# Top-k attention and ELU feed-forward: the products with the values placed behind the first feed-forward share of a step, and one subtraction for both rows

## The chip, the core and the metric

The kernel runs on one core of a Trainium2 chip. The core has five engines with queues of their own: TensorE (PE in the profile, PEld for its weight loads), VectorE (DVE), ScalarE (ACT), GpSimd (POOL) and SyncE (SP), which here only starts DMAs. The metric is the device time of one execution in microseconds (us). The engines work through their queues in the order in which the program was written, and wait for one another by semaphores.

## The reference

Inputs are `q`, `k`, `v` of shape (8, 8, 576, 64) (batches, heads, rows, head size), `w_in` (512, 2048) and `w_out` (2048, 512). Cut to what matters:

```
scores = q @ k.T / sqrt(64)                      # per batch and head, 576 x 576
kth    = 32nd largest of each row
scores = where(scores >= kth, scores, -1e9)
scores = scores - max(scores, -1)
attn   = exp(scores); attn /= sum(attn, -1) + 1e-9
x      = (attn @ v), heads side by side          # 4608 x 512
h      = x @ w_in
g      = where(h > 0, h, exp(min(h, 0)) - 1)     # ELU
out    = g @ w_out                               # 4608 x 512
```

## The kernel before, in words

**Steps.** A *tile* is 128 query rows of a batch (five per batch; the fifth, the remainder, holds the 64 last rows and takes two head pairs at once). A *step* is one tile with two heads, `i` = 0 and 1 (a remainder step packs four heads' 64 rows into the same shape); there are 144. The tile `sc` holds the scores of a step as 128 x 2 x 576. The main loop runs over `n` and works on four steps at once: it makes the scores of step `n + 2` (`scores`, products L329 into PSUM `scps`, ACT's copies L337), selects the threshold of step `n` on DVE (`select`), masks step `n - 1` (`mask`) and normalises it at the end (`normalise`), and turns step `n - 2` (`turn`).

**Select** finds the 32 largest of each row: four times MAX8 (L349, L363) with three MATCH_REPLACE8 between (L356). `u.first` (tile `m1`) keeps the first eight, `u.last` (tile `m4`) the last eight, so that `u.last[:, i, 7]` is the 32nd largest and `u.first[:, i, 0]` the largest. It is a generator with four passes; `next(passes)` emits one.

**Mask** works on one head `i`: POOL forms `gap`, the threshold less the largest score (L384, one column), ACT applies a very steep Prelu around the threshold (L385) and then Exp with `gap` as bias and the row's sum as by-product (L386). In the first steps (`early`, up to step 8) ACT forms `gap` itself (L382). Four-column tile `den` holds the two sums and the two gaps.

**Normalise** is POOL alone: L396 to L401 make the reciprocals on 128 x 2, L403 multiplies the two rows of 576.

**Turn** transposes the nine 128-column chunks of `sc` on PE (L422, five in `eps` and `scps`, then four in `eps`), and ACT copies them to `et` (L423, three copies). When the last tile of a group (one or two tiles of one head pair) is turned, the group goes onto `closing`, and the next step calls **attend**: ten products with the values (L448, PSUM `avps`; twenty for the remainder), each a 128 x 64 weight, and ACT's copy to `xT` (L475, in `finish`). When a block of one to three tiles is complete, its feed-forward pieces join the list `ffn`.

**Feed-forward pieces.** A block has 16 hidden pieces and four projection pieces per tile. A hidden piece is four products (L523, PSUM `hps`, two buffers); where a PSUM bank is full ACT takes Relu of both signs (L533, L536), and for every pair of pieces Exp (L538) and, later on, a Copy with bias -1 (L542); POOL adds the halves (L493; in the first steps and for the last block DVE does, L495), the *gate*, some shares later. A projection piece is four products (L551, PSUM `ops`); after the fourth piece ACT copies the result (L560) and SP writes it out (L563). In the profile each of these products shows as two records, so that a piece is "x8", the values of a group "x20" or "x40" and the scores of a step "x8" or "x16".

**Feed.** `feed(n, 0.25)` is called four times a step. It closes gates that are old enough and emits as many pieces as a plan of shares allows, made before the loop from estimated costs. The order of instructions on each engine is just the order of these calls, since the kernel schedules by hand. Buffers: five `sc`, two `et`, four of each small tile; `avps` and `eps` share two PSUM buffers, and the last chunk of the first transposes lies in the bank of the second head's scores.

The start of a step reads (L686 to L693):

```python
        if ahead and n > 1:
            scores(ahead)
        while closing:
            attend(closing.pop(0))
        next(passes)
        feed(n, 0.25)
        if prev:
            mask(prev, 0, n <= tight)
```

Of the kernel before, what the change touches and what calls it, by code (L numbers as in the profile page):

```python
# [9 lines left out]
ALU = mybir.AluOpType  # L10
FP32 = mybir.dt.float32
# [69 lines left out]
def kernel(  # L81
# [9 lines left out]
    nc = tc.nc  # L91
    P = nc.NUM_PARTITIONS
# [18 lines left out]
    def pool(name, bufs, **kw):  # L111
        return ctx.enter_context(tc.tile_pool(name=name, bufs=bufs, **kw))
# [6 lines left out]
    small = pool("small", 4)  # L119
# [8 lines left out]
    early = raws.enter_context(tc.tile_pool(name="early", bufs=1))  # L128
# [73 lines left out]
    def settle():  # L202

        if decode or late or blocks[0].left or any(x[3] == 0 for x in ffn):
            return
        raws.close()
        late["f"] = ctx.enter_context(tc.tile_pool(name="f", bufs=2))
        late["g"] = ctx.enter_context(tc.tile_pool(name="g", bufs=2))
        late["x"] = ctx.enter_context(tc.tile_pool(name="xt", bufs=2))
        late["in"] = ctx.enter_context(tc.tile_pool(name="in", bufs=2))  # L210
# [100 lines left out]
    def turn_qk(whole=False):  # L311
        while turning:
            if next(turning[0], turning) is turning:
                turning.pop(0)
            elif not whole:
                return
# [3 lines left out]
    def scores(u):  # L320

        u.sc = scpool.tile([P, 2, S], FP32, tag="sc", name="sc")
        q0 = (QUERIES if u.t.b == 0 else S) + u.t.qt * P
        for half in range(2):
            for h, i, rows in u.heads:
                kq = kqT[u.t.b, h // 2]
                part = slice(i * D, (i + 1) * D)
                k0 = (KEYS if i == 0 and u.t.b == 0 else 0) + half * HS
                nc.tensor.matmul(  # L329
                    wide[i][rows, half, 0:HS],  # L330
                    kq[part, q0 : q0 + u.t.ql],
                    kq[part, k0 : k0 + HS],
                    start=True,
                    stop=True,
                )
        for i in range(2):
            nc.scalar.activation(  # L337
                u.sc[:, i, :].rearrange("p (a s) -> p a s", a=2),
                wide[i][:, :, 0:HS], AF.Copy, scale=scale,
            )  # L340

    def select(u, more=False):

        u.first = small.tile([P, 2, 8], FP32, tag="m1", name="m1")
        u.last = small.tile([P, 2, 8], FP32, tag="m4", name="m4")
        cur = [u.sc[:, i, :] for i in range(2)]
        found = [u.first[:, i, :] for i in range(2)]
        for i in range(2):
            nc.vector.max(found[i], cur[i])  # L349
        if more:  # L350
            hook()
        yield
        wk = [wkpool.tile([P, S], FP32, tag=f"wk{i}", name="wk")[:] for i in range(2)]
        for r in range(TOP_K // 8 - 1):
            for i in range(2):
                nc.vector.match_replace(wk[i], found[i], cur[i], TAKEN)  # L356
            cur = wk
            for i in range(2):
                if r < TOP_K // 8 - 2:
                    found[i] = small.tile([P, 8], FP32, tag=f"m{i}", name="m")[:]  # L360
                else:
                    found[i] = u.last[:, i, :]
                nc.vector.max(found[i], cur[i])  # L363
            hook()
            yield

    def mask(u, i, early=False):

        if u.masked:
            return
        if i == 0:
            u.den = small.tile([P, 4], FP32, tag="den", name="den")
        u.masked = i == 1
        sc, low, top = u.sc[:, i, :], u.last[:, i, 7:8], u.first[:, i, 0:1]
        gap = u.den[:, 2 + i : 3 + i]  # L380
        if early:
            nc.scalar.activation(gap, top, AF.Prelu, scale=-1.0, bias=low, alpha=1.0)  # L382
        else:
            nc.gpsimd.tensor_tensor(gap, low, top, ALU.subtract)  # L384
        nc.scalar.activation(sc, sc, AF.Prelu, scale=-1.0, bias=low, alpha=1.0 / STEEP)  # L385
        nc.scalar.activation(  # L386
            sc, sc, AF.Exp, scale=-STEEP, bias=gap, accum_out=u.den[:, i : i + 1]
        )
# [43 lines left out]
    def attend(g):  # L432
        t = g.tiles[0]
        ps = ps_t.tile([P, JP], FP32, tag="t", name="avps")
        n = P if t.rem else sum(x.ql for x in g.tiles)
        for k in range(2 if t.rem else 1):
            hp = 2 * g.hp + k if t.rem else g.hp
            vt = vT[t.b, hp]
            for c in range(J + 1):
                for i in range(2):  # L440
                    chunk = J if c == J else i * (J + 1) + c
                    w = g.et[:, chunk, :, :].rearrange("p a q -> p (a q)")
                    cols = slice(0, n)
                    if t.rem:
                        c0 = R * (k if i == 0 else 1 - k)
                        w = w[:, c0 : c0 + R]
                        cols = slice(k * R, (k + 1) * R)
                    nc.tensor.matmul(  # L448
                        ps[i * D : (i + 1) * D, cols],
                        vt[:, 2 * J + i if c == J else i * J + c, :],  # L450
                        w,
                        start=(c == 0),
                        stop=(c == J),
                    )
        if t.rem:
            finish(t.block, 2, slice(2 * g.hp, 2 * g.hp + 2), t.cols,
                   ps[:, 0:n].rearrange("p (a q) -> p a q", a=2))
            return
        c0 = 0
        tiles = list(g.tiles)  # L460
        while tiles:
            blk, lo, parts = tiles[0].block, tiles[0].cols.start, 0
            while tiles and tiles[0].block is blk:
                parts += 1
                hi = tiles.pop(0).cols.stop
            finish(blk, parts, g.hp, slice(lo, hi), ps[:, c0 : c0 + hi - lo])
            c0 += hi - lo
# [15 lines left out]
    def close_gates(keep=0, upto=None):  # L483

        while gates:
            put, group, dst, n, apart = gates[0]
            if put > place[0] - keep if upto is None else group > upto:
                return  # L490
            gates.pop(0)
            if apart:
                nc.gpsimd.tensor_tensor(dst, n, dst, ALU.add)  # L493
                continue
            nc.vector.scalar_tensor_tensor(  # L495
                out=dst, in0=n, scalar=-1.0, in1=dst, op0=ALU.add, op1=ALU.add
            )
# [81 lines left out]
    blocks, tight = [], 2 * NHP  # L579
    for b in range(B):  # L580
# [28 lines left out]
        for qts in order:  # L609
# [3 lines left out]
            for qt in qts:  # L613
                n = len(steps)
# [24 lines left out]
    def feed(n, share):  # L639

        place[0] += 1
        close_gates(2 if n > tight + 3 else 6)
        fed["at"] = max(fed["at"], n)
        ahead = [(w - fed["sum"]) / (x - fed["at"]) for x, w in due if x > fed["at"]]
        if ahead:
            fed["over"] += max(0.0, share * min(ahead))
        fed["at"] += share
        while ffn and decoded[0] >= ffn[0][1] and 0.5 * ffn[0][0] <= fed["over"]:
            cost, _, piece, _ = ffn.pop(0)
            fed["over"] -= cost  # L650
            fed["sum"] += cost
            piece()
            settle()
# [22 lines left out]
    def step(n):  # L676
        return steps[n] if 0 <= n < NS else None
# [3 lines left out]
    for n in range(NS + 3):  # L681
        for fn, args in todo.pop(n, []):
            fn(*args)
        ahead, cur, prev, done = step(n + 2), step(n), step(n - 1), step(n - 2)
        passes = select(cur, n < tight) if cur else iter(range(4))
        if ahead and n > 1:  # L686
            scores(ahead)
        while closing:
            attend(closing.pop(0))
        next(passes)  # L690
        feed(n, 0.25)
        if prev:
            mask(prev, 0, n <= tight)  # L693
        if n > 1:
            turn_qk()
        next(passes)
        feed(n, 0.25)
        if done:
            turn(done, main)
            turn(done, rest)  # L700
        if prev:
            mask(prev, 1, n <= tight)
        next(passes)
        feed(n, 0.25)
        if done:
            turn(done, other)
        next(passes)
        if prev:
            normalise(prev)
        feed(n, 0.25)  # L710
        turn_qk(True)
        if n < 2:
            scores(ahead)
# [36 lines left out]
```

## Time and profile before

| what | us |
|---|---|
| median of 3 runs | 1633.88 (1632.33 to 1633.99) |
| the profiled execution, its own time | 1633.17 |
| span of that execution's instructions | 1631.4 |
| PE busy | 1569.5 (96%) |
| DVE busy | 1454.4 (89%) |
| ACT busy | 1174.6 (72%) |
| POOL busy | 711.6 (44%) |

The span runs from the first to the last instruction; the execution's own time has 1.8 us more around it. "Busy" of PE is modelled: products are pipelined, and one that stands in the pipeline and waits can count as busy. A line `PE avps L448 <- ACT et L423: 19.7, 26, 2.4` of the waits means that PE sat idle for 19.7 us in total, 26 times, 2.4 us at most, before a product into `avps` of line 448, until ACT's write of `et` at line 423. In a timeline line the first number is the start and the second the length of a run of like instructions; idle time before it stands in brackets. The granted clock of TensorE is 1.00 in nearly all of the span after the first 125 us.

### The profile page before, as it was taken

What the parts mean: (1) busy time and instruction counts of PE and PEld (TensorE: products, weight loads), DVE (VectorE), ACT (ScalarE), POOL (GpSimd) and SP (SyncE); (2) the same over time, 40 slices, a digit from 0 to 9 for tenths busy, and PEclk for the clock granted to TensorE, in tenths of its full rate; (3) what the DMA queues carried; (4) which work ended last, traced back from release to release, by engine and by line L of the source; (5) the groups of instructions that cost most, each with busy time, mean ns of one, the idle gap of its engine ahead of it and who ended that gap; (6) DMA issues with size and microseconds to landing.
All of it is one profiled execution on the core that took longest, in us unless ns stands there. A gap on an engine that the chain in (4) does not pass through costs nothing.

```text
span 1631.4 us, 25301 instructions
## 1 busy us (share of the span) xinstructions
PE 1569.5 (96%) x8276; PEld 1004.7 (62%) x8276; DVE 1454.4 (89%) x2980; ACT 1174.6 (72%) x2369; POOL 711.6 (44%) x1535
## 2 busy tenths in 40 slices
PE   4789999999999999999999999999999999999999
PEld 2477666766665757555566666655557575755564
DVE  7899999999999999999999699999999599998000
ACT  6987777877776868778577786868668695958521
POOL 4983345444443444444344443535435353534300
PEclk9779999999999999999999999999999999999999
DMA  8521310012100310022000200012100201000000
GB/s 243 187 79 36 65 37 1 7 22 45 43 1 19 54 37 7 7 40 46 23 8 15 55 21 25 1 28 45 36 14 1 43 1 36 1 13 1 7 14 13
DMA packets 188035, 56.17 MB, mean 34 GB/s; under 512 B 178176, under 2 KB 179200, under 8 KB 187904
## 3 DMA queue, kind: packets, MB, share of 16 engines
q1 hardware_dynamic: 186704, 54.26, 14.1%
q8 instruction: 66, 1.08, 0.3%
q14 instruction: 65, 0.53, 0.1%
q10 hardware_dynamic: 1200, 0.30, 0.1%
HBM read 45.09 MB, written 9.44 MB: 33 GB/s over the span
## 4 chain that ended last, share of the span: by engine, by line
PE 74%; ACT 14%; DVE 5%; POOL 3%; issue 1%; SPq 1%; DMA 1%; ACTq 0%; DVEq 0%; POOLq 0%
PE ops L551 29%; PE hps L523 22%; PE avps L448 10%; PE scps L329 7%; PE eps L422 5%; ACT sc L386 3%; DVE wk L356 2%; ACT sc L385 2%; ACT et L423 2%; DVE m L363 2%; ACT n L542 1%; ACT n L533 1%; ACT n L538 1%; ACT gT L536 1%; POOL sc L403 1%
## 5 line engine op out<-in xcount | busy, mean ns | idle before, releaser
L363 DVE MAX8 m<-wk 128x8 f32<-128x576 f32 x864 | 611.2, 751 | 0.3 <-POOL den L384 0.3
L523 PE MATMUL hps<-xT,w_in 128*128 128x256 f32 (+2 forms) x2432 | 542.9, 373 | 0.0
L551 PE MATMUL ops<-w_out,gT 128*128 128x512 f32 x1152 | 522.5, 598 | 0.0
L523 PEld LDWEIGHTS hps<-xT,w_in 128*128 128x128 f32 x2432 | 404.9, 192 | 97.4 <-issue 25.4
L356 DVE MATCH_REPLACE8 wk<-m,wk 128x576 f32<-128x576 f32 x576 | 424.5, 747 | 0.0
L551 PEld LDWEIGHTS ops<-w_out,gT 128*128 128x128 f32 x1152 | 208.6, 190 | 231.7 <-issue 230.6
L396 POOL TENSOR_SCALAR dene<-den 128x2 f32<-128x2 f32 x144 | 32.5, 225 | 693.1 <-ACT sc L386 692.5
L386 ACT ACTIVATE sc<-sc,den 128x576 f32<-128x576 f32 x288 | 223.4, 776 | 66.1 <-POOL den L384 44.4
L385 ACT ACTIVATE sc<-sc,m 128x576 f32<-128x576 f32 x288 | 225.0, 781 | 9.6 <-DVE m L363 9.5
L337 ACT ACTIVATE sc<-scps 128x576 f32<-128x576 f32 x288 | 170.9, 646 | 77.8 <-PE scps L329 77.8
L448 PE MATMUL avps<-et,vT 128*64 128x256 f32 (+2 forms) x2080 | 205.6, 328 | 20.1 <-ACT et L423 19.7
L329 PE MATMUL scps<-kqT 64*128 64x288 f32 (+1 forms) x1280 | 199.9, 443 | 25.1 <-ACT kqT L305 12.6
L349 DVE MAX8 m<-sc 128x8 f32<-128x576 f32 x288 | 202.6, 747 | 20.6 <-ACT sc L337 20.6
L403 POOL TENSOR_SCALAR sc<-sc,rec 128x576 f32<-128x576 f32 x288 | 213.5, 751 | 14.9
L423 ACT COPY et<-eps 128x512 f32<-128x512 f32 x288 | 164.6, 571 | 66.2 <-PE eps L422 66.2
L356 DVE MATCH_REPLACE8 wk<-m,sc 128x576 f32<-128x576 f32 x288 | 212.2, 746 | 0.0
L448 PEld LDWEIGHTS avps<-et,vT 128*64 128x64 f32 x2080 | 128.0, 141 | 101.0 <-ACT et L423 34.2
L422 PEld LDWEIGHTS eps<-ident,sc 128*128 128x128 f32 x1152 | 143.4, 143 | 72.4 <-issue 53.9
L493 POOL TENSOR_TENSOR gT<-n,gT 128x512 f32<-128x512 f32 (+1 forms) x120 | 166.2, 1385 | 38.0 <-ACT n L542 38.0
L422 PE MATMUL eps<-ident,sc 128*128 128x128 f32 x1152 | 174.1, 277 | 0.1
L329 PEld LDWEIGHTS scps<-kqT 64*128 64x128 f32 (+1 forms) x1280 | 107.0, 182 | 102.5 <-issue 46.2
L533 ACT ACTIVATE n<-hps 128x512 f32<-128x512 f32 (+1 forms) x156 | 87.0, 558 | 58.0 <-PE hps L523 57.1
(45 smaller groups left out, 988.5 us busy)
## 6 DMA issues: line engine op xcount, KB each, us to landing
raw<-in_moe_w_in_dram SPq DMA_DIRECT2D x16, 512.0 KB, 4.9
vT<-in_v_dram SPq DMA_DIRECT2D x64, 128.0 KB, 2.4
raw<-in_moe_w_out_dram SPq DMA_DIRECT2D x16, 512.0 KB, 3.8
out_dram<-osb SPq DMA_DIRECT2D x32, 256.0 KB, 2.0
kin<-in_k_dram SPq DMA_DIRECT2D x112, 72.0 KB, 2.4
qin<-in_q_dram SPq DMA_DIRECT2D x112, 72.0 KB, 2.5
kin<-in_k_dram SPq DMA_DIRECT2D x8, 128.0 KB, 4.7
vT<-in_v_dram SPq DMA_DIRECT2D x64, 16.0 KB, 2.2
```

Source lines behind the costliest of these rows:

```text
L329: nc.tensor.matmul(wide[i][rows, half, 0:HS], kq[part, q0 : q0 + u.t.ql], kq[part, k0 : k0 + HS], start=True, stop=True,)
L349: nc.vector.max(found[i], cur[i])
L356: nc.vector.match_replace(wk[i], found[i], cur[i], TAKEN)
L363: nc.vector.max(found[i], cur[i])
L385: nc.scalar.activation(sc, sc, AF.Prelu, scale=-1.0, bias=low, alpha=1.0 / STEEP)
L386: nc.scalar.activation(sc, sc, AF.Exp, scale=-STEEP, bias=gap, accum_out=u.den[:, i : i + 1])
L403: nc.gpsimd.tensor_scalar(u.sc[:, i, :], u.sc[:, i, :], rec[:, i : i + 1], 1.0, ALU.mult, ALU.mult)
L422: nc.tensor.transpose(ps[:, c * P : (c + 1) * P], sc[:, c0 : c0 + P], ident[:])
L423: nc.scalar.copy(g.et[:, chunks, u.at, :], ps[:, 0 : n * P].rearrange("p (c q) -> p c q", c=n),)
L448: nc.tensor.matmul(ps[i * D : (i + 1) * D, cols], vt[:, 2 * J + i if c == J else i * J + c, :], w, start=(c == 0), stop=(c == J),)
L523: nc.tensor.matmul(blk.h[:, f % bank, :], w_in[:, i, f * P : (f + 1) * P], blk.xT[:, i, 0:n_tok], start=(i == 0), stop=(i == NC - 1),)
L551: nc.tensor.matmul(blk.o[:], blk.gT[f // NG][:, f % NG, s * P : (s + 1) * P], w_out[:, f, :], start=(f == 0), stop=(f == NF - 1),)
```

## The change

The call of `attend` moves from the place before the first pass and the first feed of a step to the place behind them. The subtraction that forms the gaps is taken out of `mask` for all steps that are not early and becomes one POOL operation on two columns, in a new function `spread`, called once a step ahead of the first pass. The tile `den` is then made in `spread`. Lines from 367 on move down by 7, those behind the mask's subtraction by 5, and those behind the moved call by 7 again; the prediction keeps to the numbers of the kernel before.

```diff
+    def spread(u):
+
+        u.den = small.tile([P, 4], FP32, tag="den", name="den")
+        nc.gpsimd.tensor_tensor(
+            u.den[:, 2:4], u.last[:, :, 7], u.first[:, :, 0], ALU.subtract
+        )
+
     def mask(u, i, early=False):
...
-        if i == 0:
+        if i == 0 and early:
             u.den = small.tile([P, 4], FP32, tag="den", name="den")
...
         if early:
             nc.scalar.activation(gap, top, AF.Prelu, scale=-1.0, bias=low, alpha=1.0)
-        else:
-            nc.gpsimd.tensor_tensor(gap, low, top, ALU.subtract)
...
         passes = select(cur, n < tight) if cur else iter(range(4))
         if ahead and n > 1:
             scores(ahead)
+        if prev and n > tight:
+            spread(prev)
+        next(passes)
+        feed(n, 0.25)
         while closing:
             attend(closing.pop(0))
-        next(passes)
-        feed(n, 0.25)
         if prev:
             mask(prev, 0, n <= tight)
```

## The prediction

> **What bounds the kernel now.** I read the page first: its busy shares and the chain that ended last.
>
> ```profile
> PE 1569.5 (96%) x8276; PEld 1004.7 (62%) x8276; DVE 1454.4 (89%) x2980; ACT 1174.6 (72%) x2369; POOL 711.6 (44%) x1535
> PE 74%; ACT 14%; DVE 5%; POOL 3%; issue 1%; SPq 1%; DMA 1%; ACTq 0%; DVEq 0%; POOLq 0%
> ```
>
> PE and DVE are both nearly full, so an average can't say which one sets the end. The windows by stage (PE, PEld, DVE, ACT, POOL busy) can:
>
> ```profile
> 125.00:437.00 312.00, 305.26 (x1988) 209.66 (x1987) 312.00 (x641) 232.81 (x473) 137.82 (x325) 1.00 0.17 32
> 437.00:600.00 163.00, 157.76 (x842) 101.91 (x842) 160.33 (x331) 123.33 (x249) 70.90 (x157) 0.99 0.12 24
> 900.00:1300.00 400.00, 398.69 (x2027) 246.47 (x2026) 366.94 (x755) 293.72 (x594) 171.61 (x390) 1.00 0.13 27
> ```
>
> Up to 437 us DVE has no idle time, and the first Prelu of a mask (L385) starts as soon as DVE has that step's threshold: DVE sets the pace there, and nothing saved on PE is worth anything. After 437 us L385 trails DVE's last MAX8 by 3 to 29 us (12.1 us at 1441), DVE idles, and PE sets the pace, in the order in which its instructions stand. So the sum is over PE's stops after 437 us. The list of waits names those that the change can touch (us in total, times, longest):
>
> ```profile
> ACT xT L475 <- PE avps L448: 51.9, 49, 2.7
> ACT sc L386 <- POOL den L384: 44.4, 49, 4.3
> DVE kqT L283 <- PE scps L329: 36.1, 3, 16.9
> PE avps L448 <- ACT et L423: 19.7, 26, 2.4
> ```
>
> The last one is on PE. This is its longest case in the timeline (start us, length):
>
> ```profile
> 450.80 0.89 PE L329 MATMUL scps<-kqT 64*128 64x288 f32 x4
> 451.61 0.65 PE L448 MATMUL avps<-et,vT 128*64 128x256 f32 x2
> 453.55 0.63 ACT L542 ACTIVATE n<-n 128x512 f32<-128x512 f32 x1
> 454.08 0.57 ACT L423 COPY et<-eps 128x512 f32<-128x512 f32 x1
> 454.70 1.55 PE L448 MATMUL avps<-et,vT 128*64 128x256 f32 x6 [2.44 <-ACT et L423]
> ```
>
> Two records of the values product start, then PE stands until ACT, late with feed-forward work, has copied the last transposes of the step before. The wait rows show only part of this, since a record that waits in the pipeline counts as busy. So I measured each values group from its first record to the next group: undisturbed it takes 2.31 us (1.31 with remainder tiles). What is above that, over the 60 groups from 431 us on, in order: 4.43, 0.93, 1.15, 0.98, 1.60, 0.53, 0.93, 0.45, 1.69, 0.39, then 0.44, 1.40, 0.39, 1.40 at 1100, 1121, 1146 and 1482 us, six of 0.53 to 0.57 (3.28 together), 0.14, 0.79 and 0.74 in the last three, and two of 0.08: 21.8 us.
>
> **The change, part by part.** *Values behind the first share.* In the changed program's order, 40 of the 60 groups get one piece of feed-forward products between scores and values that stood behind them before; of the last three, which follow no scores, two get a projection piece in front and one a second hidden piece. A piece lasts 1.73 us (hidden, two-slot block), 2.58 (three-slot) or 3.43 (projection). No product is added: the piece only runs while ACT finishes L423. Four stops have no piece in front after the change either and stay: 1.60, 0.53, 0.39 and 0.39, 2.9 us. Of the 4.43 only 1.83 to 1.93 is covered (two-slot piece), so 2.5 stays. All others are shorter than their cover. Gain: 21.8 - 2.9 - 2.5 = 16.4 us.
>
> What PE pays: the products use three array shapes, and each change of shape has a price.
>
> ```profile
> 1390.49 0.60 PE L422 MATMUL eps<-ident,sc 128*128 128x128 f32 x4
> ...
> 1391.04 1.89 PE L523 MATMUL hps<-xT,w_in 128*128 128x256 f32 x8
> 1392.76 0.60 PE L422 MATMUL eps<-ident,sc 128*128 128x128 f32 x4
> 1393.20 1.89 PE L523 MATMUL hps<-xT,w_in 128*128 128x256 f32 x8
> 1395.02 1.24 PE L329 MATMUL scps<-kqT 64*128 64x288 f32 x8
> 1396.19 2.38 PE L448 MATMUL avps<-et,vT 128*64 128x256 f32 x20
> ```
>
> The same piece takes 1.72 us from start to next start between transposes and 1.82 ahead of scores: 0.10 for leaving the full shape. Behind scores or values it also takes 0.10 more. Before, a step goes scores, values, full shape; after it goes scores, full, values, full: one visit more. Where full products follow the values (20 groups) that is 0.20 us, out and back in. Where transposes follow (20 groups) it is 0.15: 0.10, and 0.60 for 0.55 in the transposes. Sum: 20 x 0.20 + 20 x 0.15 = 7.0 us lost. No row shows a values group behind products without a stop; one (1512.9 us) takes 2.45, which may be a wait, so 0 to 0.14 more each, at most 5.6; I take 0, since 2.45 holds a copy that ended inside it.
>
> This is where the Trainium skill speaks against the change: TensorEngine Tiling (Array Packing), Key Properties, says that changing the tiling mode drains TensorE. The rows agree and give about 0.1 us. The page gives no length; with a free drain the sum would end at 1616.8 us, with the rows' price at 1623.8.
>
> *L475 behind the piece.* ACT's copy of the values now waits later, and L385, L386 and L423 are queued behind it; POOL's normalising waits for L386 and the transposes of the next step for POOL. Projection piece, worst: before, L475 at 1440.76, first mask done 1442.77, ACT idle 1.61 until L560 at 1444.38, second mask done 1447.26, POOL's L403 done 1450.78, next transposes at 1453.4: 2.6 us spare. A shift of 3.64 loses 1.61 in ACT's gap, 2.0 arrives, under 2.6. Hidden piece: the shift of 1.93 falls into ACT's wait for products before L533 (57.1 us over 48 times). Price 0; bound below in the rivals. The hidden products that moved ahead need their PSUM freed by L536, which ACT does before the L423 they now cover, so they don't stop in its place.
>
> *One subtraction for both rows.* 272 POOL operations of 189 ns become 136 on two columns; the nearest row is L399, 128x2, 196 ns: 51.4 us become 26.7 on an engine that is 44% busy. It also stands ahead of the gate additions (L493, 1.28 or 1.83 us) of its share, which now wait behind it for DVE; nobody is listed as waiting for L493. L386's 44.4 us are ACT idle, mostly not on the chain. After 437 us three chain pieces run L493, L384, L386 (471, 553, 736 us): at most 1.24 + 1.25 + 1.78 + 3 x 0.16 = 4.8 us, largely the same stops that I counted above. I take 0. A loss: one operation waits for the second row's MAX8 (0.66 us later) before the first row's Exp, while DVE leads; the first Prelu (0.78) hides it, and up to 437 us PE's order has room.
>
> *SP and the feed.* The pieces per step stay nearly the same; a block's pieces join one share later, output DMAs move by a share, neither on the chain.
>
> Sum against the profiled execution's own 1633.17 us (span 1631.4 and 1.8 around): 1633.17 - 16.4 + 7.0 = 1623.8. The median shown is 0.7 above that execution, which would make it 1624.5; I say 1624.0, between the two and nearer to the first.
>
> **Rivals.** *The crossings and small new waits eat it.* With 2.45 for each moved group it is 1623.8 + 5.6 = 1629.4, and with the stops moved to the next ACT copy instead of removed about 1633: no change. For: ACT is 72% busy and its queue decides the stops. Against: in 900 to 1300 us it is idle for 106 of 400.
>
> *DVE holds longer.* At 601 us L385 starts only 2.96 us behind DVE; PE's net gain by then is 5.0 - 1.5 = 3.5, DVE itself gains back up to 2.67 that it idles in L283. If that lead is used up, the 3.5 is lost: 1627.5. Against: 2.96 + 2.67 is more.
>
> *Slower: masks too late.* If ACT's gap doesn't absorb the shift, all 3.64 us arrives where 2.6 are spare, and the transposes wait 1.04 in each of the 20 groups that transposes follow: +20.8, less the net gain of 9.4: 1633.17 + 11.4 = 1644.6. It decides as soon as more than 2.6 us of the shift comes through; by the timeline 2.0 does.
>
> **Chances.** Forecast 0.70, DVE 0.08, eaten 0.12, late masks 0.10. A run can tell about 0.2% (3.3 us) from no change: faster 0.78, same 0.12, slower 0.10. Low end: no price for shapes, 1617. High end: 1629.4 from the 2.45 row, stretched to 1631 for part of the eaten case; late masks and the rest stay out.
>
> **What would show it.** Right: the wait of avps for L423 after 437 us falls from 7.6 us to under 3; hidden pieces of 1.93 between scores and values; L386's wait for POOL under 20 us; L396 idle unchanged; DVE's L283 wait smaller by about the gain. Wrong: transposes of eps or scps waiting for POOL's L403 by many us, ACT's L475 waits far above 52 us with PE stopping behind them, or values groups of 2.45 and more.

## The result, and the profile after

| kernel | median (range, executions), us | ratio to before, 95% interval |
|---|---|---|
| before | 1633.24 (1632.33 to 1633.99, 4) | |
| changed | 1616.49 (1616.20 to 1616.57, 4) | 0.9897 [0.988, 0.9915] |

The change gains 16.7 us by the medians, and 16.6 us by the two profiled executions (1633.17 and 1616.54, span 1614.3). The forecast was 9.4 us, and the time lies 0.5 us below the range: sign and mechanism were right, the size wasn't. In the kernel after, the lines named in the prediction stand lower: L384 is now L370 (`spread`), L385 and L386 are L390 and L391, L403 is L408, L422 and L423 are L427 and L428, L448 is L453, L475 is L480, L523 is L528, L551 is L556.

The page of the changed kernel, its busy shares and the chain that ended last:

```profile
PE 1563.4 (97%) x8276; PEld 993.3 (62%) x8276; DVE 1454.2 (90%) x2980; ACT 1175.2 (73%) x2369; POOL 695.1 (43%) x1399
PE 71%; DVE 20%; ACT 4%; issue 2%; POOL 1%; SPq 1%; DMA 1%; DVEq 0%; ACTq 0%; POOLq 0%
```

No engine works less but POOL (136 operations fewer) and PE, whose records hold fewer hidden waits. In the chain ACT went from 14% to 4% and DVE from 5% to 20%. The chain by stage shows where: between 330 and 437 us its largest lines were PE's before (L551 26.6%, L448 13.1%, L523 12.1%), and now they are DVE's (L356 38.1%, L363 29.5%, L349 11.0%).

The windows by stage (PE, PEld, DVE, ACT, POOL busy, granted clock):

```profile
125.00:437.00 312.00, 305.99 (x1968) 209.17 (x1968) 312.00 (x642) 233.15 (x475) 132.95 (x290) 0.99 0.17 32
437.00:600.00 163.00, 161.27 (x878) 103.14 (x876) 163.00 (x337) 125.74 (x253) 70.78 (x149) 1.00 0.14 27
900.00:1300.00 400.00, 400.00 (x2064) 248.16 (x2064) 380.75 (x782) 300.48 (x607) 168.03 (x354) 1.00 0.13 27
```

From 437 to 600 us DVE now has no idle time left (2.67 us before), and PE 1.73 us where it had 5.24; from 900 to 1300 us PE is never idle. The 0.99 in the first row is a half clock from 202.6 to 206.0 us, behind a stop of 1.94 us at the scores (L329 waits for ACT's L428) that the kernel before doesn't have there. The list of waits:

```profile
ACT xT L480 <- PE avps L453: 99.1, 63, 5.2
POOL den L370 <- DVE m L363: 72.2, 40, 4.1
ACT sc L391 <- POOL den L370: 37.5, 50, 4.4
DVE kqT L283 <- PE scps L329: 23.9, 2, 16.8
PE avps L453 <- ACT et L428: 5.7, 9, 1.0
```

The last line was 19.7 us. ACT now waits 99.1 us for the values products instead of 51.9, since its copy of them stands in front of its other work. From 428 us on PE has no listed wait for that copy. The longest stop of before, at 451 us, looks like this now (timeline):

```profile
449.31 1.99 PE L528 MATMUL hps<-xT,w_in 128*128 128x256 f32 x8
451.24 0.65 PE L453 MATMUL avps<-et,vT 128*64 128x256 f32 x2
451.73 0.57 ACT L428 COPY et<-eps 128x512 f32<-128x512 f32 x1
452.35 2.37 PE L453 MATMUL avps<-et,vT 128*64 128x256 f32 x18 [0.46 <-ACT et L428]
```

The hidden piece stands between scores and values, 1.93 us from its start to the values' start, and where 2.44 us of waiting were listed, 0.46 are left. The crossings between array shapes can be read in a stretch without stops:

```profile
1315.49 1.89 PE L528 MATMUL hps<-xT,w_in 128*128 128x256 f32 x8
1317.31 1.24 PE L329 MATMUL scps<-kqT 64*128 64x288 f32 x8
1318.48 1.99 PE L528 MATMUL hps<-xT,w_in 128*128 128x256 f32 x8
1320.41 2.38 PE L453 MATMUL avps<-et,vT 128*64 128x256 f32 x20
1322.72 1.99 PE L528 MATMUL hps<-xT,w_in 128*128 128x256 f32 x8
```

From start to start the piece takes 1.82 us ahead of the scores, 1.93 us behind them, and the values behind products take 2.31 us, not 2.45: the row of 2.45 us that stood as the rival's price was a wait. All 43 groups that now stand behind full products, but the one at 451 us, take their undisturbed length.

**The sum made again, from both traces.** I measured every PE group (scores, values, transposes) from 431 us (before) and 428.5 us (after) on, from its first record to the next group's, against its undisturbed length:

| us above the undisturbed length | before | after | gone |
|---|---|---|---|
| values | 21.8 | 4.0 | 17.8 |
| scores | 4.35 | 2.5 | 1.9 |
| transposes | 3.2 | 1.1 | 2.1 |
| all | 29.4 | 7.6 | 21.8 |

The visits changed as in the order: scores followed by full shape 45 to 85 times, full shape followed by values 3 to 43, scores followed by values 57 to 17. With the prices of the prediction that is 7.0 us, which leaves 14.8; and PE reaches the transposes of step 38 (at 437.6 us before) 1.9 us earlier. Together 16.7, where the two executions differ by 16.6.

### The profile page after: what moved, and what is told of

Same layout as the page of the kernel before. It is cut to its first block, busy times and chain, and to the rows that moved or that the text cites. A ratio compares the mean times of both kernels' runs of the same rounds, so it can differ in the third digit from the quotient of the medians.

```text
span 1614.3 us, 25065 instructions
## 1 busy us (share of the span) xinstructions
PE 1563.4 (97%) x8276; PEld 993.3 (62%) x8276; DVE 1454.2 (90%) x2980; ACT 1175.2 (73%) x2369; POOL 695.1 (43%) x1399
## 4 chain that ended last, share of the span: by engine, by line
PE 71%; DVE 20%; ACT 4%; issue 2%; POOL 1%; SPq 1%; DMA 1%; DVEq 0%; ACTq 0%; POOLq 0%
PE ops L556 25%; PE hps L528 24%; DVE wk L356 9%; PE avps L453 8%; PE scps L329 8%; DVE m L363 7%; PE eps L427 6%; DVE m L349 3%; ACT sc L391 1%; DVE raw L188 1%; PE scps L427 1%; DVE kqT L283 1%; ACT sc L390 1%; ACT et L428 0%; POOL sc L408 0%
## 5 line engine op out<-in xcount | busy, mean ns | idle before, releaser
L363 DVE MAX8 m<-wk 128x8 f32<-128x576 f32 x864 | 607.1, 741 | 0.2 <-POOL den L370 0.2
L528 PE MATMUL hps<-xT,w_in 128*128 128x256 f32 (+2 forms) x2432 | 552.8, 375 | 0.0
L556 PE MATMUL ops<-w_out,gT 128*128 128x512 f32 x1152 | 522.9, 598 | 1.1 <-DVE gT L500 1.1
L528 PEld LDWEIGHTS hps<-xT,w_in 128*128 128x128 f32 x2432 | 404.7, 192 | 109.7 <-issue 38.5
L356 DVE MATCH_REPLACE8 wk<-m,wk 128x576 f32<-128x576 f32 x576 | 421.8, 737 | 0.0
L556 PEld LDWEIGHTS ops<-w_out,gT 128*128 128x128 f32 x1152 | 208.5, 190 | 235.1 <-issue 231.5
L401 POOL TENSOR_SCALAR dene<-den 128x2 f32<-128x2 f32 x144 | 33.0, 229 | 662.1 <-ACT sc L391 661.5
L391 ACT ACTIVATE sc<-sc,den 128x576 f32<-128x576 f32 x288 | 223.4, 776 | 50.4 <-POOL den L370 37.5
L390 ACT ACTIVATE sc<-sc,m 128x576 f32<-128x576 f32 x288 | 225.0, 781 | 22.3 <-DVE m L363 22.2
L329 PE MATMUL scps<-kqT 64*128 64x288 f32 (+1 forms) x1280 | 200.2, 443 | 27.7 <-ACT et L428 14.5
L408 POOL TENSOR_SCALAR sc<-sc,rec 128x576 f32<-128x576 f32 x288 | 214.4, 755 | 14.9 <-POOL rec L406 0.2
L349 DVE MAX8 m<-sc 128x8 f32<-128x576 f32 x288 | 201.3, 738 | 17.6 <-ACT sc L337 17.6
L356 DVE MATCH_REPLACE8 wk<-m,sc 128x576 f32<-128x576 f32 x288 | 210.8, 737 | 0.0
L428 ACT COPY et<-eps 128x512 f32<-128x512 f32 x288 | 164.6, 571 | 52.2 <-PE eps L427 52.1
L453 PE MATMUL avps<-et,vT 128*64 128x256 f32 (+2 forms) x2080 | 188.5, 325 | 5.8 <-ACT et L428 5.7
L427 PEld LDWEIGHTS eps<-ident,sc 128*128 128x128 f32 x1152 | 141.0, 143 | 67.8 <-issue 48.0
L427 PE MATMUL eps<-ident,sc 128*128 128x128 f32 x1152 | 174.9, 277 | 1.0 <-ACT xT L480 0.5
L329 PEld LDWEIGHTS scps<-kqT 64*128 64x128 f32 (+1 forms) x1280 | 106.7, 181 | 105.2 <-issue 45.6
L453 PEld LDWEIGHTS avps<-et,vT 128*64 128x64 f32 x2080 | 119.3, 140 | 83.8 <-issue 39.0
```

The costliest lines, as they stand in the source:

```text
L329: nc.tensor.matmul(wide[i][rows, half, 0:HS], kq[part, q0 : q0 + u.t.ql], kq[part, k0 : k0 + HS], start=True, stop=True,)
L391: nc.scalar.activation(sc, sc, AF.Exp, scale=-STEEP, bias=gap, accum_out=u.den[:, i : i + 1])
L408: nc.gpsimd.tensor_scalar(u.sc[:, i, :], u.sc[:, i, :], rec[:, i : i + 1], 1.0, ALU.mult, ALU.mult)
L427: nc.tensor.transpose(ps[:, c * P : (c + 1) * P], sc[:, c0 : c0 + P], ident[:])
L453: nc.tensor.matmul(ps[i * D : (i + 1) * D, cols], vt[:, 2 * J + i if c == J else i * J + c, :], w, start=(c == 0), stop=(c == J),)
L528: nc.tensor.matmul(blk.h[:, f % bank, :], w_in[:, i, f * P : (f + 1) * P], blk.xT[:, i, 0:n_tok], start=(i == 0), stop=(i == NC - 1),)
```

## The experiments

Each ratio is to runs of the kernel before on the same chip. "Steps" are counted by the transposes: the start of step m's first transposes against that of before is how far PE is ahead there. The code shows the lines that matter; `...` stands for others.

**1. The move alone.** In the kernel before, only the two blocks change places; the masks keep their two subtractions.

```diff
-        while closing:
-            attend(closing.pop(0))
         next(passes)
         feed(n, 0.25)
+        while closing:
+            attend(closing.pop(0))
```

> Only the values move behind the first feed-forward share; the two subtractions stay where they were, one per head. Theory A (PE's stops behind ACT's copies, in the values and in the scores and transposes around them, are what the move removes): nearly the whole gain, 1616.5 to 1618 us. Theory B (the 7 us more than forecast come from the single early subtraction, since ACT waited 44 us for POOL's L384): about 1624 us.

Measured: 1616.40 us (1616.27 to 1617.05), ratio 0.9896 [0.9881, 0.9911]. The move is all of the gain.

**2. The single subtraction alone.** The changed kernel with the values back at their old place.

```diff
+        while closing:
+            attend(closing.pop(0))
         next(passes)
         feed(n, 0.25)
-        while closing:
-            attend(closing.pop(0))
```

> Only the single subtraction ahead of the first pass; the values stay ahead of the first share. Theory A: 1632 to 1634 us, no difference that counts, though ACT's wait for the gap falls. Theory B: about 1626 us.

Measured: 1631.00 us (1629.25 to 1632.59, 11 executions), ratio 0.9983 [0.9975, 0.9992], 1 us below what was expected. By itself it gains 2 to 3 us, and the trace shows PE ahead by 0.5 us at step 38, 1.0 at step 60, 1.7 at step 100 and 2.5 at step 143. Its groups show where: the six stops of 0.53 to 0.57 us at values groups are 0.43 to 0.48 here, as if ACT came to its copies (L428) about 0.1 us earlier each time. Where the values stand behind a piece, these six stops are gone, and nothing is left to shorten: with the move the subtraction is worth nothing (experiment 1), as the prediction had it.

**3. The change before step 40 only, and from step 40 on only.** This asks whether PE's stops count while DVE leads.

```diff
...
+        new = n < 40        # the other kernel: n >= 40
-        if prev and n > tight:
+        if prev and n > tight and new:
             spread(prev)
+        while closing and not new:
+            attend(closing.pop(0))
```

Beside these lines, a mask whose step had no `spread` forms its gaps with the two subtractions of before.

> Both parts of the change in the steps below 40, the order of before from step 40 on. Theory A: the transposes of step 38 come 1.9 us earlier as in the changed kernel, PE keeps that lead, and the time is 1630.5 to 1632 us. The forecast's reading (DVE leads there, nothing saved on PE counts): 1633.2 us.

> The order of before in the steps below 40, both parts of the change from step 40 on. Theory A: 1617.5 to 1619.5 us, the full gain less about 2 us that the first steps bring. The forecast's reading: 1616.5 us, the same as the changed kernel.

Measured: from step 40 on 1618.33 us (1618.28 to 1618.38), 0.9906 [0.9893, 0.992]: 1.84 us slower than the whole change, so the first 40 steps are worth that much on top of the rest, not nothing. The first 40 alone: 1635.44 us (1632.1 to 1637.09, 11 executions), 1.0007 [0.9998, 1.0016], no gain, and above both of the times that were expected. By its trace PE is 1.29 us ahead at step 38 and 0.74 at step 100; most of what it then loses lies in one place. The order of before had a hidden piece between transposes and values at 1510.2 us; in this kernel the pieces stand differently by then, and the values follow the transposes at once (timeline and windows of this kernel, where L457 is the values and L432 the copy):

```profile
1508.77 0.60 PE L431 MATMUL eps<-ident,sc 128*128 128x128 f32 x4
1509.30 0.65 PE L457 MATMUL avps<-et,vT 128*64 128x256 f32 x2
1511.88 3.56 PE L457 MATMUL avps<-et,vT 128*64 128x256 f32 x18 [1.93 <-ACT et L432]
...
1509.50:1512.90 3.40, 1.47 (x12) 0.73 (x12) 0.39 (x1) 2.23 (x6) 1.77 (x6) 1.00 0.00 0
1512.90:1516.30 3.40, 3.40 (x14) 1.62 (x11) 0.00 (x0) 0.37 (x1) 3.30 (x5) 0.50 0.00 0
```

A stop of 1.93 us is listed, and in the 3.4 us behind it the granted clock is 0.50: 3.76 us in all at this group, where before lost 0.14. So this kernel doesn't measure the first 40 steps by its time; the other one does.

**4. One group alone.** Only the values of step 42 (the stop of 4.43 us at 451 us) go behind the first share.

```diff
-        while closing:
+        while closing and n != 42:
             attend(closing.pop(0))
         next(passes)
         feed(n, 0.25)
+        while closing:
+            attend(closing.pop(0))
```

> The kernel before, with the values moved behind the first share in step 42 alone, the step of the 4.43 us stop at 451 us, after which the granted clock was 0.50 for 3.4 us. Theory C (that stop is a wait of some 2.9 us and a half clock of some 1.5 us that follows from it): no half clock there any more, and the transposes of step 40 come 3.4 to 3.8 us earlier than in the kernel before; the time 1630 us. The forecast's reading (a cover of 1.93 us takes off 1.93, less 0.2 for shapes): 1.7 us earlier, 1632 us.

Measured: 1630.51 us (1630.16 to 1631.03, 10 executions), ratio 0.9977 [0.9967, 0.9987]. Behind this group PE is 2.9 us ahead of the kernel before, and in front of it 0.2 us late: 3.1 us from one piece of 1.93 us. The time is as the theory of the half clock expected it; the 3.1 us is under its 3.4 to 3.8: the stop falls from 4.43 to 1.16 us, and the two crossings take 0.2 of that. Windows around it, first of before and then of this kernel:

```profile
450.70:454.10 3.40, 1.56 (x8) 0.61 (x6) 3.40 (x8) 3.27 (x8) 1.54 (x6) 0.99 0.00 0
454.10:457.50 3.40, 2.80 (x14) 1.66 (x16) 3.40 (x8) 1.64 (x4) 2.99 (x5) 0.50 0.00 0
```

```profile
450.70:454.10 3.40, 3.40 (x16) 2.24 (x16) 3.40 (x8) 3.28 (x7) 1.45 (x5) 1.00 0.00 0
454.10:457.50 3.40, 2.87 (x21) 1.63 (x20) 3.40 (x8) 2.03 (x5) 3.09 (x6) 1.00 0.00 0
```

And the values records behind the stop, in the timelines of before and of this kernel:

```profile
454.70 3.72 PE L448 MATMUL avps<-et,vT 128*64 128x256 f32 x18 [2.44 <-ACT et L423]
```

```profile
453.73 0.65 PE L448 MATMUL avps<-et,vT 128*64 128x256 f32 x2
454.90 2.37 PE L448 MATMUL avps<-et,vT 128*64 128x256 f32 x18 [0.53 <-ACT et L423]
```

Before, the clock was halved from 454.1 to 457.5 us, and the same eighteen records took 3.72 instead of 2.37 us: 1.35 of the 4.43 was a slow clock, not waiting. What waited was 3.08, and 3.08 less the piece's 1.93 is 1.15, beside 1.16 measured. The half clock at this place stands in the profiles of before and of experiments 2 and 3 (first 40 steps), which keep the stop, and in none of the nine profiles with a piece in front of it.

The Trainium skill, TensorE: Matmul & The Clock Gate (Part 1, What's actually happening), says that TensorE falls back to half clock after an idle window of about 3.4 us, by a window that runs freely. The length agrees (454.1 to 457.5), and so does the free window: the stretches of one clock in the trace of before last 3.41, 6.83, 20.48 or 334.51 us, whole multiples of 3.413. "Idle" is too narrow: in the window ahead PE was busy for 1.56 of 3.40 us here and for 1.47 in experiment 3. No bound on the busy time comes out of these traces: with 1.82 us of 3.40 the clock stayed full (experiment 7, 416.4 to 419.8 us), and with 2.26 it was halved (experiment 5, 220.8 to 224.2 us).

**5. Values at their old place where the pieces are projections.** From step 70 on, where none of the last four shares had a hidden piece, the values stay ahead of the first share: 13 groups without a stop worth naming. Transposes follow them, so with the change each pays for one more visit of the full shape.

```diff
...
+        if 70 <= n < NS and not any(hidden_last):
+            while closing:
+                attend(closing.pop(0))
         next(passes)
         feed(n, 0.25)
         while closing:
             attend(closing.pop(0))
```

> The changed kernel, but from step 70 on the values stand ahead of the first share again wherever the last four shares held no hidden piece: 13 groups, all in front of projection pieces and none with a stop. Forecast's price of the shapes (0.15 us each): 1.95 us faster than the changed kernel, 1614.5 us. Rival (the price is hidden, or was only an artefact of how products end in the trace): 1616.5 us, no difference.

Measured: 1614.40 us (1614.24 to 1614.65), ratio 0.9881 [0.9867, 0.9896], 2.09 us less than the changed kernel. The stops stay as they were (7.5 against 7.6 us), and 13 visits are gone: 0.16 us each. That is the prediction's price of the array shapes, 0.15 where transposes follow, and a cost of this order that can be avoided.

**6. Values still later where no piece came.** From step 40 on the values wait for the second share where the first had no piece in or just behind a hidden stretch; then the same together with experiment 5.

```diff
...
+        wait = 40 <= n < NS and any(hidden_last) and not fed["piece"]
-        while closing:
+        while closing and not wait:
             attend(closing.pop(0))
...
         next(passes)
         feed(n, 0.25)
+        while closing:
+            attend(closing.pop(0))
```

> The changed kernel, but from step 40 on, where the first share of a step emits no piece in or just after a hidden stretch, the values wait for the second share. Covers the stops that the changed kernel still has at 630, 651, 753 and 1131 us of its span (1.61, 0.44, 0.44, 0.44 us) at 6 further changes of shape of 0.15: 2.0 us faster than the changed kernel, 1614.5 us. Rival (values that come later delay the masks and PE stops elsewhere): 1616.5 us or slower.

> Both of the last two edits: if the terms add, 4 us faster than the changed kernel, 1612.5 us. If they share a limit (DVE's lead), about 1614.5 us.

Measured: alone 1616.73 us (1616.24 to 1617.23), 0.9895 [0.9881, 0.991], no gain; together 1614.44 us (1614.13 to 1614.66), 0.9881 [0.9866, 0.9896], the same as experiment 5. The stops that it aims at go (at 630 us 1.61, and three of 0.44), but six more visits cost 0.9, and a wait that the changed kernel doesn't have from 428 us on stands in the list of waits of PE:

```profile
PE eps L427 <- ACT xT L480: 1.4, 2, 0.7
```

Behind the second share the values stand directly ahead of transposes, and `avps` and `eps` share two PSUM buffers. ACT's copy of the values comes late, behind the mask and the work of a hidden piece, and the transposes wait for the buffer. Timeline of the first kernel:

```profile
1132.95 2.38 PE L453 MATMUL avps<-et,vT 128*64 128x256 f32 x20
...
1135.26 0.66 PE L427 MATMUL eps<-ident,sc 128*128 128x128 f32 x4
1135.75 0.27 PE L427 MATMUL scps<-ident,sc 128*128 128x128 f32 x1
1136.30 0.35 ACT L480 COPY xT<-avps 128x256 f32<-128x256 f32 x1
...
1136.71 0.66 PE L427 MATMUL eps<-ident,sc 128*128 128x128 f32 x4 [0.68 <-ACT xT L480]
```

**7. The mask ahead of the values.** The slower rival said that ACT's later copy of the values makes the masks late. Here the first head's mask is written ahead of the values, so that the copy is not in its way.

```diff
+        if prev and n > tight:
+            mask(prev, 0)
         while closing:
             attend(closing.pop(0))
-        if prev:
-            mask(prev, 0, n <= tight)
+        if prev and n <= tight:
+            mask(prev, 0, True)
```

> The changed kernel with the first head's mask (Prelu and Exp on ACT) written ahead of the values products from step 9 on, so that ACT's copy of the values no longer stands in front of it; the same work otherwise. Theory (the later copy of the values costs nothing, since the masks have room to the next transposes): 1616 to 1617.5, no gain beside 1616.5; ACT's wait of xT for avps falls from 99 us, since two ACT operations fill it. Rival (late masks hold up the transposes, as the prediction's slower case has it): faster by over 1 us, with the PE stops at transposes smaller. A third way: the copy of the values, now 1.56 us later, holds up a projection piece or the transposes' copies: slower by 0.5 to 2 us.

Measured: 1617.31 us (1617.28 to 1617.67), ratio 0.9904 [0.9887, 0.992]. The third way, 0.8 us slower. From step 40 to step 143 PE gains 11.0 us on before, as in the changed kernel (10.9): the masks were not late there. The loss of 1.2 us is all there by step 38: the mask waits for DVE's threshold, the copy of the values waits behind it, and the transposes wait for the copy:

```profile
416.05 0.78 ACT L390 ACTIVATE sc<-sc,m 128x576 f32<-128x576 f32 x1 [4.81 <-DVE m L363]
...
417.83 0.35 ACT L480 COPY xT<-avps 128x256 f32<-128x256 f32 x1
418.23 0.66 PE L427 MATMUL eps<-ident,sc 128*128 128x128 f32 x4 [1.58 <-ACT xT L480]
```

**8. Experiments 5 and 6 together, the late values in steps 40 to 79 only.** This keeps the stop at 630 us away and leaves out the later groups, that of 1135 us among them.

```diff
-        wait = 40 <= n < NS and any(hidden_last) and not fed["piece"]
+        wait = 40 <= n < 80 and any(hidden_last) and not fed["piece"]
```

> The changed kernel, with the values ahead of the first share from step 70 on wherever none of the last four shares had a hidden piece (13 groups, as in e5_hidden), and in steps 40 to 79 alone behind the second share where the first had no piece (as in e7_late, without its later groups, the one at 1131 us among them). If the terms add: e5_hidden's 1614.4, less the stop of 1.6 us at 630 us, plus the visits of the array shapes in these groups (0.15 each): 1613.0 to 1613.4. Rival (the pace at these steps is set by DVE's lead, so that a stop taken away there is given back): 1614.2 to 1614.8, as e5_hidden.

Measured: 1613.20 us (1612.94 to 1613.75), ratio 0.9879 [0.9865, 0.9894], the time expected if the terms add: 1.2 us less than experiment 5, and the fastest version here, 3.3 us below the changed kernel. Experiment 5 ran on another chip, and the two ratios can't be told apart; the traces can: from step 56 to step 80 PE gains 1.07 us on that of experiment 5, and elsewhere from step 40 on nothing. Two terms that the sum left out nearly cancel, which was luck: the stops of 0.44 at 651 and 753 us go too, and of the wait for `xT` one case of 0.7 us is left, at 638 us.

## Why the prediction was right and wrong

**Right.** The gain comes from PE's stops at the values, covered by a piece that had to run anyway: the wait of `avps` for the copies after 437 us fell from 7.6 to 1.4 us (under 3 was said), the pieces take the 1.93 us, and DVE's wait at L283 fell by 12.2 us. The two crossings cost what the rows of before gave, 0.15 us where transposes follow (experiment 5) and 0.20 where full products do (1.93 for 1.73 in the piece, above); the row of 2.45 us, the price of the rival in which they eat the gain, was a wait. The subtraction is worth nothing beside the move (1 and 2). The later masks cost nothing from step 40 on (7).

**Wrong, in three terms of the sum, all too small.**

- *Only the values groups were counted.* Scores and transposes had 7.5 us of stops of their own in the same stage, 4.0 of which went with the values' stops. "The sum is over PE's stops after 437 us" was right as a rule; the measuring behind it was done for one kind of group. Which of the moved pieces removed which of these was not tried one by one.
- *The stop at 451 us.* "Of the 4.43 only 1.83 to 1.93 is covered" took all of it for waiting. 1.35 us were half clock that the stop itself brought on, and they went with it: 3.3 gone, 1.4 more than the sum had (experiment 4).
- *The first 38 steps.* "Nothing saved on PE is worth anything" rested on L385 starting with DVE's threshold. Up to step 29 (344 us) the traces bear this out: DVE's thresholds come at the same times in both kernels, to 0.1 us, and PE's lead comes and goes, 3.8 us at step 14, -0.8 at step 15, none at step 24. From step 30 on the reading fails. In the kernel before, L385 of step 31 starts 3.5 us behind the end of the last MAX8 (timeline), and that of steps 34 and 36 2.0 and 2.2 us:

```profile
353.29 1.42 DVE L363 MAX8 m<-wk 128x8 f32<-128x576 f32 x2
358.21 0.76 ACT L385 ACTIVATE sc<-sc,m 128x576 f32<-128x576 f32 x1
```

And where L385 starts at once, as in step 37, it shows that the masks follow DVE, not that PE's transposes do. Their start behind POOL's normalised rows (L403, L408 after) is the row to read, first before and then after:

```profile
423.65 1.48 POOL L403 TENSOR_SCALAR sc<-sc,rec 128x576 f32<-128x576 f32 x2
427.79 0.60 PE L422 MATMUL eps<-ident,sc 128*128 128x128 f32 x4
```

```profile
421.98 1.48 POOL L408 TENSOR_SCALAR sc<-sc,rec 128x576 f32<-128x576 f32 x2
424.70 0.60 PE L427 MATMUL eps<-ident,sc 128*128 128x128 f32 x4
```

Before, the transposes of step 37 come 2.7 us after the rows are ready, with the change 1.2: PE was late by its own order there. The rows are ready 1.7 us earlier too, with DVE's threshold at 416.5 us in both, so ACT and POOL had been late as well. PE is 3.1 us ahead in this step and 1.9 in the next; the kernel without the change in this stage lost 1.84 (experiment 3).

Together 4.0 + 1.4 + 1.9 = 7.3, the difference between 9.4 and the 16.6 measured, to 0.1.

**Three other steps.** "L386's wait for POOL under 20 us" was wrong, 37.5 us: the early operation is itself late, since POOL waits for DVE in front of it (72.2 us at L370, 16.3 at L384 before). It didn't matter to the time. Nor did "L396 idle unchanged", which was wrong too: POOL's idle time there fell from 693.1 to 662.1 us, as part of its waiting now lies in front of L370. "DVE holds longer" did happen: DVE is busy for all 163 us between 437 and 600, and L390 starts with DVE again at steps 50 to 56. But PE's lead shrinks there by 0.5 us only, from 9.05 at step 50 to 8.58 at step 58, not by the 3.5 of that rival; by then the stops of this stage had been covered.

## What to carry to other kernels

An engine that is busy without a gap need not set the pace: DVE was, up to 437 us, and yet the chain ran mostly over PE from about 330 us on. Where PE sets the end, measure every kind of group from its start to the next start, since waits inside "busy" records count as well; and look at the granted clock behind each long stop, because a stop can cost its length and a slow clock on top. An independent piece of work between a product and the one that waits for its copies removes the stop if it is as long; where there is no stop it only pays for the changes of array shape, so place it group by group. Before a copy is moved behind a wait, see whose buffer it frees.

## What the runs showed of the hardware

- A stop of about 2 to 3 us was followed by half clock for 3.4 us where little of the 3.4 us window ahead was work (1.56 and 1.47 us busy): the three profiles that keep the stop at 451 us have it there, the nine with the stop covered don't. How much work keeps the clock full is open: 1.82 us did, 2.26 didn't.
- A change between the array shapes of these products costs about 0.1 us (a piece takes 1.72, 1.82 or 1.93 us with none, one or two), and a group placed between full products instead of behind the scores 0.15 to 0.20 us; taking 13 of them back gained 2.09 us.
- Where the stop at 451 us is covered, the executions scatter less: with that one group moved 1630.16 to 1631.03 us over 10 executions (experiment 4), the kernel before on the same chip 1631.99 to 1635.22 over 13. That the clock is the reason is not shown.
